# An attention and expert-layer kernel: the product with v in two column tiles, and the sums of the exponentials on GpSimd

## The chip, the cores and the metric

The kernel runs on one core of a Trainium2 chip. The metric is the device time of one execution in microseconds (us). TensorE (PE, with PEld for its weight loads) multiplies matrices into PSUM; VectorE (DVE), ScalarE (ACT) and GpSimd (POOL) work element by element; SyncE (SP) issues most of the transfers (DMA).

## What is computed

Clustered attention, followed by two multiplicative layers. The part that matters here is the end of the attention:

```python
mask = q_assign[:, :, :, None] == k_assign[:, :, None, :]
scores = scale * np.matmul(q, k.transpose(0, 1, 3, 2))
scores = np.where(mask, scores, -1000000000.0)
scores = scores - np.max(scores, axis=-1, keepdims=True)
attn = np.exp(scores)
attn = attn / (np.sum(attn, axis=-1, keepdims=True) + 1e-09)
return np.matmul(attn, v).astype(np.float32)
```

There are 2 batches of 8 heads, so 16 heads, with 768 queries and keys and 64 columns of v each. The result, as 1536 rows of 512, goes through `(x @ w1) * (x @ w2) @ w3 @ w_out` and then `softplus(x @ w_in) @ w_out2`. Everything is float32.

## The kernel before

The program has three stages. A preparation reads the first heads. A loop over slots (`for s in range(NSLOT + ML + AL)`, L897) does the attention, six slots to a head (QC = 6), 96 slots of work and ten to fill and empty the pipeline; beside it runs the product of w3 and w_out, in steps of a table (`w_step`), and the preparation of the next pair of heads (`steps`). Then come the two layers, l1 and l2 first (L965), l3 and l4 after.

In slot s the loop issues, in this order: the minimum products of slot s (`mx_pe`) and their reduction on VectorE (`mx_red`); the score products of slot j = s - 9 (`st_pe`) into the bank `sb`, and their exponential on ScalarE (`st_exp`) into a tile E; the product with v of slot a = s - 10 (`av_pe`) into the bank `avb`. Each of `mb`, `sb` and `avb` is one buffer, so the next slot's products wait until its reader has finished. E has two buffers.

A slot of scores covers 256 keys (two tiles i of 128) and 384 queries, one half hf; three slots make a half. The array holds 128 columns for `av_pe`: 64 of v and 64 of ones (`load_v` sets them by a memset on GpSimd), so that one half of the rows of `avb` holds the product and the other the sum of the exponentials:

```python
for i in range(2):
    nc.tensor.matmul(avbank[:, :HALF], V[g][:, 2 * kp + i, :], e[:, i, :],
        start=(kp == 0 and i == 0), stop=(kp == 2 and i == 1))
```

`av_ev` copies `avb` to a tile t on ScalarE, twice a head. The sums then go through DRAM: `r_ev` issues on SyncE sd<-t (twice), r<-sd, then rd<-r behind a reciprocal of 128 x 6 on VectorE, then R<-rd, which spreads the reciprocals over 64 rows. `x_norm` multiplies t by R on GpSimd, into XT.

The order of the work is written out by hand in the loop; each engine runs its own instructions in order, and waits for what the others must have finished. Behind the loop the weights of l1 are decoded (ACT, DVE, POOL in turn, `feed.take`) and XT is split into tiles xs (`split_x`), which share the four buffers of the pool xp with the tiles of v.

Of the kernel before, what the change touches and what calls it, by code (L numbers as in the profile page):

```python
# [8 lines left out]
F32 = mybir.dt.float32  # L9
# [18 lines left out]
def fused_kernel(ctx: ExitStack, tc, q, k, v, centroids, w1, w2, w3, wo, w_in, w_o2, out):  # L28
# [6 lines left out]
    nc = tc.nc  # L35
    B, H, S, D = q.shape
# [3 lines left out]
    QC = S // P  # L40
    HALF = S // 2
# [29 lines left out]
    cpool = pool(ctx, "cpool")  # L71
    dma_in = nc.sync.dma_start
# [51 lines left out]
    nc.vector.memset(ones, 1.0)  # L124
    half_c = cpool.tile([P, 1], F32, name="half_c")
    nc.vector.memset(half_c, 0.5)
    wfirst = cpool.tile([P, NCL], F32, name="wfirst")
    for c in range(NCL):
        nc.vector.memset(wfirst[:, c : c + 1], float(NCL - c))
# [37 lines left out]
                yield slice(lo - o, hi - o), XT[b][:, c, lo - b * S : hi - b * S]  # L167

    w12e = pool(ctx, "w12e", bufs=4, side="right")
    ep = pool(es_att, "ep", bufs=2, side="right")  # L170
    sp = pool(es_att, "sp", bufs=2, side="right")
    w3p = pool(es_att, "w3p", bufs=2, side="right")
    drp = pool(es_att, "drp", bufs=2, space=DRAM)


    xp = pool(ctx, "xp", bufs=4)
# [384 lines left out]
    NWSTEP = 3 * NW + 10  # L561

    def load_v(pi):

        if pi < NPAIR:
            b, h0 = divmod(2 * pi, H)
            for j in range(2):
                t = xp.tile([P, QC, 2 * D], F32, tag="x", name=f"v{pi}_{j}")
                nc.gpsimd.memset(t[:, :, D * (1 - j) : D * (2 - j)], 1.0)
                dma_in(  # L570
                    t[:, :, D * j : D * j + D], v[b, h0 + j].rearrange("(p c) d -> p c d", p=P)
                )
                V[2 * pi + j] = t


    PE = {
# [13 lines left out]
    NH = B * H  # L590
    NSLOT = NH * QC
    ML = 9
    AL = 1
    MN, E, TT, R = {}, {}, {}, {}


    def mx_pe(s):
# [24 lines left out]

    def st_pe(j):
        g, r = divmod(j, QC)
        hf, kp = divmod(r, 3)
        qs = slice(hf * HALF, (hf + 1) * HALF)
        for i in range(2):
            ks = slice((2 * kp + i) * P, (2 * kp + i + 1) * P)
            for n in range(2):
                nc.tensor.matmul(  # L630
                    sbank[:, i, :HALF], KT[g][: P - 31 * n, n, ks],
                    QT[g][: P - 31 * n, n, qs], start=(n == 0), stop=(n == 1),
                )

    def st_exp(j):
# [3 lines left out]
    def av_pe(j):  # L639

        g, r = divmod(j, QC)
        kp = r % 3
        e = E.pop(j)
# [6 lines left out]
    def av_ev(u):  # L650
        g, hf = divmod(u, 2)
        j = g % 2
        t = TT[u] = sp.tile([P, HALF], F32, tag="t", name=f"t{u}", bufs=5)
        act_copy(t, avbank[:, :HALF])
        if hf == 0:
            R["s", g] = drp.tile([2, HALF], F32, tag="sd", name=f"sd{g}")
        o = D * (1 - j)
        nc.sync.dma_start(R["s", g][hf : hf + 1, :], t[o : o + 1, :])

    def r_ev(g, i):  # L660

        pi, j = divmod(g, 2)
        if i == 0:
            R["t", g] = sp.tile([P, 2, QC], F32, tag="r", name=f"r{g}")
            nc.sync.dma_start(
                R["t", g][:, 0], R.pop(("s", g)).rearrange("h (a x) -> (h a) x", x=QC)
            )
        elif i == 1:
            t = R.pop(("t", g))
            nc.vector.tensor_scalar(  # L670
                out=t[:, 0], in0=t[:, 0], scalar1=1e-9, scalar2=None, op0=ALU.add
            )
            nc.vector.reciprocal(t[:, 1], t[:, 0])
            R["d", g] = drp.tile([2, HALF], F32, tag="rd", name=f"rd{g}")
            nc.sync.dma_start(R["d", g].rearrange("h (a x) -> (h a) x", x=QC), t[:, 1])
        else:
            if j == 0:
                R[pi] = sp.tile([P, S], F32, tag="R", name=f"R{pi}")
            nc.sync.dma_start(
                R[pi][D * j : D * j + D, :],  # L680
                R.pop(("d", g)).rearrange("h n -> (h n)").partition_broadcast(D),
            )

    def x_norm(u):
        g, hf = divmod(u, 2)
# [158 lines left out]
    with tc.manual_schedule():  # L844
        act_dma = nc.scalar.dma_start
        load_qk(0, [0])
        load_qk(0, [1], act_dma)
        nc.scalar.preload_act_table_set("natural_log_exp_and_others")
        centroid_load()
        for _ in range(3):  # L850
            w_load()
        centroid_prep()
        t1_pe(0, 0)
        t1_pe(0, 1)
        t1_ev(0, 0)
# [24 lines left out]
        assign(0, 1)  # L880
        w_step(0, "A")
        wk[0] = 1
        back_pe(0)
        back_ev(0)
        m_dma(0, 0, act_dma)
        m_dma(0, 1, act_dma)
        for r in range(-20, -2 * QC):
            steps(PE, r + 2 * QC)
            steps(EV, r + 2 * QC)
            if r % 2 == 0:  # L890
                w_next()
                w_next()
        while wk[0] < W0:
            w_next()
        load_v(0)
        load_v(1)
        for s in range(NSLOT + ML + AL):  # L897
            j = s - ML
            a = j - AL
            if s < NSLOT:  # L900
                mx_pe(s)
                mx_red(s)
            if s and s % QC == 0 and s <= NSLOT:
# [19 lines left out]
            for g in range(NH):
                r = s - (ML + AL + QC * g + QC - 1)
                if r in (2, 4, 6):
                    r_ev(g, r // 2 - 1)
                if r == 8:
                    x_norm(2 * g)
                    x_norm(2 * g + 1)
# [5 lines left out]
    av_ev(2 * NH - 1)  # L935
    for g in range(NH):
        r0 = NSLOT + ML + AL - (ML + AL + QC * g + QC - 1)
        for r in (2, 4, 6):
            if r >= r0:
                r_ev(g, r // 2 - 1)  # L940
        if 8 >= r0:
            x_norm(2 * g)
            x_norm(2 * g + 1)
# [167 lines left out]
```

## Time and profile before

| | us |
|---|---|
| median of 3 runs (lowest, highest) | 858.82 (856.37, 859.01) |
| the profiled execution | 859.42 |
| its span | 857.6 |
| of it before the loop's steady part, 0 to 55 | 55 |
| the loop over heads, 55 to 387 | 332 |
| the layers, 387 to 857.6 | 470.6 |

Over the whole span PE is busy 94%, PEld 74%, DVE 58%, ACT 46% and POOL 28%. Matmuls are pipelined, so the record of one overlaps the next; what a matmul costs in a row of them is read from the chain of waits, which gives each piece only the time that it adds. A line such as L645 names the place in the program. A row of a group gives the instruction, what it writes and reads, its shape and count, the busy time, the mean duration in ns, and the idle time just before it with what ended it.

### The profile page before, as it was taken

The page shows a single profiled execution, that of the slowest core. Times are in us where ns is not written, and L with a number is a line of the kernel's source. Part 1 is how long each engine was busy: PE and PEld are TensorE (multiplying, and loading weights), DVE is VectorE, ACT ScalarE, POOL GpSimd, SP SyncE. Part 2 cuts the span into 40 slices and gives each one's busy share as a digit, 9 for nine tenths or more (in the row PEclk, how much of TensorE's full clock was granted, in tenths as well). Part 3 has the DMA queues.
Part 4 walks back from the last instruction along what each step waited for, and adds up shares of the span by engine and source line. Part 5 has one row for each costly group of instructions (what it writes and reads, how often), then busy time and mean ns, then how long its engine had stood idle before and what let it go on. Part 6 is the DMA issues. An engine that isn't in the chain of part 4 may idle for free.

```text
span 857.6 us, 10092 instructions
## 1 busy us (share of the span) xinstructions
PE 802.5 (94%) x3553; PEld 637.9 (74%) x3553; DVE 495.6 (58%) x823; ACT 396.4 (46%) x683; POOL 243.6 (28%) x229
## 2 busy tenths in 40 slices
PE   4269999998999999989999999999999999999997
PEld 3157777776777777758888888887877788888886
DVE  5675657674776664438543254553988644454442
ACT  3324444554443444455443235454564644455443
POOL 2241214261424111135411113231344222222221
PEclk9979999998999999999999999999999999999999
DMA  8585474577445364025511114340120000001001
GB/s 211 136 185 147 101 178 115 147 164 171 120 111 120 84 157 109 15 69 183 170 49 50 50 50 147 99 147 1 50 74 1 23 28 1 0 1 50 1 1 50
DMA packets 77827, 76.40 MB, mean 89 GB/s; under 512 B 46416, under 2 KB 62928, under 8 KB 77776
## 3 DMA queue, kind: packets, MB, share of 16 engines
q1 hardware_dynamic: 72880, 74.17, 32.3%
q10 hardware_dynamic: 4896, 1.57, 1.0%
q8 instruction: 28, 0.46, 0.2%
q14 instruction: 23, 0.19, 0.1%
HBM read 50.41 MB, written 3.24 MB: 63 GB/s over the span
## 4 chain that ended last, share of the span: by engine, by line
PE 78%; DVE 9%; ACT 3%; SPq 3%; DMA 3%; issue 2%; POOL 1%; ACTq 0%; DVEq 0%; POOLq 0%
PE avb L645 13%; PE rb L793 8%; PE sb L793 8%; PE sb L630 7%; PE sb L999 6%; PE mb L1042 6%; PE rb L999 5%; PE rb L515 5%; PE mb L815 4%; PE mb L600 4%; PE rb L1042 3%; PE avb L1042 3%; PE avb L815 2%; PE rb L815 2%; PE rb L353 2%
## 5 line engine op out<-in xcount | busy, mean ns | idle before, releaser
L609 DVE TENSOR_REDUCE mn<-mb 128x1 f32<-128x768 f32 x96 | 91.8, 956 | 95.4 <-PE mb L600 95.2
L645 PE MATMUL avb<-E,v 128*128 128x384 f32 x384 | 143.1, 495 | 1.4 <-ACT t L61 1.3
L66 POOL TENSOR_TENSOR u<-u,t 128x512 f32<-128x512 f32 x48 | 68.5, 1427 | 170.1 <-DVE u L1022 170.1
L637 ACT ACTIVATE E<-sb 128x768 f32<-128x768 f32 x96 | 77.7, 810 | 68.7 <-PE sb L630 67.2
L630 PE MATMUL sb<-q,k 128*128 128x384 f32 (+1 forms) x384 | 92.2, 363 | 9.2 <-ACT E L637 9.2
L645 PEld LDWEIGHTS avb<-E,v 128*128 128x128 f32 x384 | 71.9, 193 | 30.8 <-ACT t L61 4.4
L600 PE MATMUL mb<-k,q 128*128 128x384 f32 x192 | 70.0, 447 | 16.6 <-DVE mn L609 16.1
L630 PEld LDWEIGHTS sb<-q,k 128*128 128x128 f32 (+1 forms) x384 | 67.6, 195 | 16.2 <-ACT E L637 13.0
L999 PE MATMUL sb<-ys,wh_i 128*128 128x512 f32 x192 | 64.1, 395 | 3.6 <-ACT t L1010 2.3
L600 PEld LDWEIGHTS mb<-k,q 128*128 128x128 f32 x192 | 36.0, 201 | 36.7 <-DVE mn L609 21.2
L999 PE MATMUL rb<-ys,wh_i 128*128 128x512 f32 x192 | 63.4, 392 | 0.0
L793 PE MATMUL rb<-xs,wh 128*128 128x512 f32 x192 | 61.6, 392 | 0.0
L793 PE MATMUL sb<-xs,wh 128*128 128x512 f32 x192 | 61.6, 392 | 0.0
L1012 DVE TENSOR_SCALAR u<-t 128x512 f32<-128x512 f32 x48 | 21.4, 446 | 66.8 <-ACT t L1011 66.8
L66 POOL TENSOR_TENSOR wl_o<-d_o,wh_o 128x512 fp32r<-128x512 f32 x16 | 21.6, 1350 | 121.2 <-ACT wh_o L61 121.2
L69 DVE TENSOR_TENSOR gl<-u,gh 128x512 fp32r<-128x512 f32 x48 | 39.6, 825 | 19.6 <-ACT gh L61 19.1
L692 POOL TENSOR_TENSOR xT<-t,R 64x384 f32<-64x384 f32 x32 | 34.7, 1102 | 46.8 <-DMA R<-rd 37.1
L1021 ACT ACTIVATE u<-u 128x512 f32<-128x512 f32 x48 | 30.4, 633 | 35.6 <-DVE t L1018 35.4
L999 PEld LDWEIGHTS sb<-ys,wh_i 128*128 128x128 f32 x192 | 35.9, 188 | 13.6 <-ACT t L1010 3.4
L333 POOL MEMSET k<- 1x768 f32 x16 | 11.8, 744 | 107.6 <-issue 83.2
L999 PEld LDWEIGHTS rb<-ys,wh_i 128*128 128x128 f32 x192 | 36.1, 188 | 8.0
L793 PEld LDWEIGHTS sb<-xs,wh 128*128 128x128 f32 x192 | 36.1, 188 | 7.8
(175 smaller groups left out, 1798.7 us busy)
## 6 DMA issues: line engine op xcount, KB each, us to landing
w3r<-in_moe_w_dram SPq DMA_DIRECT2D x16, 512.0 KB
w12r<-in_moe_w_dram SPq DMA_DIRECT2D x16, 512.0 KB
wir<-in_moe_w_in_dram SPq DMA_DIRECT2D x16, 512.0 KB
wor<-in_moe_w_out_dram SPq DMA_DIRECT2D x16, 512.0 KB
q<-H SPq DMA_DIRECT2D x16, 384.0 KB
w3r<-in_moe_w_out_dram SPq DMA_DIRECT2D x8, 512.0 KB
k<-H SPq DMA_DIRECT2D x16, 192.0 KB
k<-L SPq DMA_DIRECT2D x16, 192.0 KB
```

Of the source, the lines that this page charges most:

```text
L66: nc.gpsimd.tensor_tensor(out=o, in0=i, in1=hi, op=ALU.subtract)
L69: return nc.vector.tensor_tensor(out=o, in0=i, in1=hi, op=ALU.subtract)
L515: nc.tensor.matmul(m, a[:, ks], bb, start=(mc == 0 and x == 0), stop=(mc == NK - 1 and x == 2))
L600: nc.tensor.matmul(mbank[:, hf, :HALF], QT[g][:, 0, c * P : (c + 1) * P], KT[g][:, 0, hf * HALF : (hf + 1) * HALF], start=True, stop=True,)
L609: nc.vector.tensor_reduce(out=MN[g][:, c : c + 1], in_=mbank[:, :, :HALF], op=ALU.min, axis=AX.XY)
L630: nc.tensor.matmul(sbank[:, i, :HALF], KT[g][: P - 31 * n, n, ks], QT[g][: P - 31 * n, n, qs], start=(n == 0), stop=(n == 1),)
L637: nc.scalar.activation(E[j], sbank[:, :, :HALF], AF.Exp, scale=-1.0)
L645: nc.tensor.matmul(avbank[:, :HALF], V[g][:, 2 * kp + i, :], e[:, i, :], start=(kp == 0 and i == 0), stop=(kp == 2 and i == 1),)
L793: nc.tensor.matmul(bk[:, :BLK], a[:, sl], bb, start=(n == 0), stop=(n == 3 * CC - 1))
L815: nc.tensor.matmul(ybank[e][:, :BLK], a[:, es], bb, start=(fc == 0 and n == 0), stop=(fc == NFC - 1 and n == 2),)
L999: nc.tensor.matmul(hbank[(bl * NF2 + fc) % 4][:, :BLK], a[:, sl], bb, start=(n == 0), stop=(n == 3 * CC - 1))
L1042: nc.tensor.matmul(ob, a[:, sl], bb, start=(fc == 0 and n == 0), stop=(fc == NF2 - 1 and n == 2),)
```

## The change

The product with v uses v alone, 64 columns wide. A slot now covers 128 keys and all 768 queries, and its two products, one for each half of the queries, write rows 0 to 63 and 64 to 127 of `avb`. The memsets of ones in v go. The sums are made apart: GpSimd adds the six E of a head (`es_add`, five adds of 128 x 768), TensorE multiplies the result with a tile of ones (`sum_pe`, two products of 64 columns a head), and ScalarE copies them and adds 1e-9 (`sum_ev`). The reciprocals are taken on all 128 rows, in three instructions of 128 columns a head (`r_ev`). The DRAM tiles and the five transfers a head go. E has four buffers; the sums share the pool xp with v and xs.

```diff
-    ep = pool(es_att, "ep", bufs=2, side="right")
+    ep = pool(es_att, "ep", bufs=4, side="right")
...
+            t = xp.tile([P, 2, QC, D], F32, tag="x", name=f"v{pi}")
+            dma_in(t, v[b, h0 : h0 + 2].rearrange("h (p c) d -> p h c d", p=P))
             for j in range(2):
-                t = xp.tile([P, QC, 2 * D], F32, tag="x", name=f"v{pi}_{j}")
-                nc.gpsimd.memset(t[:, :, D * (1 - j) : D * (2 - j)], 1.0)
...
+                V[2 * pi + j] = t[:, j]
...
     def st_pe(j):
         g, r = divmod(j, QC)
-        hf, kp = divmod(r, 3)
-        qs = slice(hf * HALF, (hf + 1) * HALF)
-        for i in range(2):
-            ks = slice((2 * kp + i) * P, (2 * kp + i + 1) * P)
-            for n in range(2):
+        ks = slice(r * P, (r + 1) * P)
+        for n in range(2):
+            for i in range(2):
                 nc.tensor.matmul(
                     sbank[:, i, :HALF], KT[g][: P - 31 * n, n, ks],
-                    QT[g][: P - 31 * n, n, qs], start=(n == 0), stop=(n == 1),
+                    QT[g][: P - 31 * n, n, i * HALF : (i + 1) * HALF],
+                    start=(n == 0), stop=(n == 1),
                 )
...
         for i in range(2):
             nc.tensor.matmul(
-                avbank[:, :HALF], V[g][:, 2 * kp + i, :], e[:, i, :],
-                start=(kp == 0 and i == 0), stop=(kp == 2 and i == 1),
-            )
...
+                avbank[D * i : D * i + D, :HALF], V[g][:, r, :], E[j][:, i, :],
+                start=(r == 0), stop=(r == QC - 1),
+            )
+
+    def es_add(j):
...
+        nc.gpsimd.tensor_tensor(out=ES[g], in0=a, in1=e, op=ALU.add)
...
+    def sum_pe(g):
...
+        for i in range(2):
+            nc.tensor.matmul(m[D * i : D * i + D, :HALF], ones, e[:, i, :], start=True, stop=True)
+
+    def sum_ev(g):
+        m = R.pop(("b", g))
+        R[g] = sp.tile([P, HALF], F32, tag="R", name=f"R{g}")
+        nc.scalar.activation(R[g], m[:, :HALF], AF.Identity, bias=epscol[:, 0:1])
+        give(m)
...
+        t = R[g][:, i * P : (i + 1) * P]
+        nc.vector.reciprocal(t, t)
...
+    def head_end(g, r, part):
+
+        if part == 0:
+            if r == 1:
+                av_ev(g)
+            if r == 3:
+                sum_ev(g)
+        elif part == 1:
+            if r == 2:
+                sum_pe(g)
+        else:
+            if r in (3, 4, 5):
+                r_ev(g, r - 3)
+            if r == 7:
+                x_norm(g, 0)
+                x_norm(g, 1)
...
             if 0 <= a:
                 av_pe(a)
+                es_add(a)
+            for x in ends:
+                head_end(*x, 1)
```

Here r counts the slots since the last product of head g.

On TensorE, late in the loop where no w3 products are left, three slots read like this before (mb holds the minimum products, sb the scores, avb the product with v; x2 and x4 count instructions, the last figures are rows out x columns):

```order
L600 MATMUL mb_98<-k15_2661,q15_2660 128x384 x2
L630 MATMUL sb_97<-q13_2366,k13_2367 128x384 x4
L645 MATMUL avb_99<-E82_2842,v6_1_2507 128x384 x2
L600 MATMUL mb_98<-k15_2661,q15_2660 128x384 x2
L630 MATMUL sb_97<-q14_2575,k14_2576 128x384 x4
L645 MATMUL avb_99<-E83_2857,v6_1_2507 128x384 x2
```

and like this now, around the sums of head 12:

```order
L625 MATMUL sb_99<-q13_2347,k13_2348 128x384 x4
L639 MATMUL avb_101<-E78_2757,v6_2487 64x384 x2
L597 MATMUL mb_100<-k14_2554,q14_2553 128x384 x2
L625 MATMUL sb_99<-q13_2347,k13_2348 128x384 x4
L639 MATMUL avb_101<-E79_2771,v6_2487 64x384 x2
L666 MATMUL rb2_104<-es12_2698,ones_65 64x384 x2
L597 MATMUL mb_100<-k15_2639,q15_2638 128x384 x2
```

The products with v have 64 rows out and stand between products of 128, and once a head two more of 64 follow them.

On GpSimd, in the same part of the loop, a head had the two products of `x_norm`, the memsets of v and one memset of k before:

```order
L692 TENSOR_TENSOR xT1_2467<-t20_2495,R5_2691 64x384
L692 TENSOR_TENSOR xT1_2467<-t21_2568,R5_2691 64x384
L569 MEMSET v7_0_2745 128x6x64
L569 MEMSET v7_1_2748 128x6x64
L692 TENSOR_TENSOR xT1_2467<-t22_2631,R5_2691 64x384
```

Now five adds stand between the products of two heads:

```order
L686 TENSOR_TENSOR xT1_2429<-t10_2547,R10_2596 64x384 x2
L655 TENSOR_TENSOR es12_2698<-E72_2667,E73_2681 128x768
L655 TENSOR_TENSOR es12_2698<-es12_2698,E74_2694 128x768
L655 TENSOR_TENSOR es12_2698<-es12_2698,E75_2716 128x768
L655 TENSOR_TENSOR es12_2698<-es12_2698,E76_2731 128x768
L655 TENSOR_TENSOR es12_2698<-es12_2698,E77_2744 128x768
L686 TENSOR_TENSOR xT1_2429<-t11_2675,R11_2706 64x384 x2
```

Each add follows its E, and frees it.

On TensorE at the end of the loop, l1 (xs times wh and wl) followed the last product with v before:

```order
L793 MATMUL rb0_100<-xs0_0_3061,wh1_0_3051 128x512
L645 MATMUL avb_99<-E95_3019,v7_1_2748 128x384 x2
L793 MATMUL sb_97<-xs0_0_3061,wh0_0_2931 128x512
L793 MATMUL sb_97<-xs0_0_3061,wl0_0_2932 128x512
L793 MATMUL sb_97<-xs0_0_3061,wh0_0_2931 128x512
```

Now the sums of the last head stand within its first products:

```order
L804 MATMUL rb0_102<-xs0_0_3037,wh1_0_3027 128x512
L639 MATMUL avb_101<-E95_2995,v7_2725 64x384 x2
L804 MATMUL sb_99<-xs0_0_3037,wh0_0_2906 128x512
L666 MATMUL rb1_103<-es15_2965,ones_65 64x384 x2
L804 MATMUL sb_99<-xs0_0_3037,wl0_0_2907 128x512
```

## Rows read from the trace of the kernel before

**Rows 1.** Stretches of the span: length, each engine's busy us, clock, DMA share, GB/s

```profile
core 0: us, PE busy (x) PEld busy (x) DVE busy (x) ACT busy (x) POOL busy (x), PEclk, DMA share, GB/s
55.00:387.00 332.00, 318.77 (x1456) 244.14 (x1456) 202.25 (x336) 159.53 (x268) 97.40 (x110) 0.97 0.50 122
133.85:157.22 23.37, 23.35 (x111) 17.85 (x110) 16.13 (x28) 11.41 (x20) 6.55 (x7) 1.00 0.45 111
177.07:194.53 17.46, 17.01 (x80) 12.43 (x79) 15.55 (x26) 10.45 (x18) 12.19 (x11) 1.00 0.60 145
221.44:245.02 23.58, 23.56 (x113) 17.84 (x112) 18.26 (x32) 11.46 (x21) 6.55 (x7) 1.00 0.50 122
196.00:207.00 11.00, 7.65 (x23) 5.12 (x23) 4.39 (x9) 3.31 (x6) 2.45 (x4) 0.75 0.65 167
```

**Rows 2.** Chain of waits, pieces of the loop: start us, us, what

```profile
145.72 0.44 PE rb L496 x4
...
295.27 2.78 PE rb L515 x12
...
358.52 0.35 PE mb L600 x2
358.87 0.70 PE sb L630 x4
359.57 1.29 PE avb L645 x4
360.86 0.11 PE rb L616
```

**Rows 3.** Timeline of PE and PEld, same slots: start, duration, instruction, count

```profile
142.79 0.81 PE L600 MATMUL mb<-k,q 128*128 128x384 f32 x2
...
143.09 0.19 PEld L600 LDWEIGHTS mb<-k,q 128*128 128x128 f32 x1
143.26 0.08 PEld L616 LDWEIGHTS rb<-identF,mn 128*6 128x6 f32 x1
...
359.41 1.45 PE L645 MATMUL avb<-E,v 128*128 128x384 f32 x4
```

**Rows 4.** DVE groups (busy, mean ns), then L465's durations, least, median, most, 55:387

```profile
L673 DVE RECIPROCAL r<-r 128x6 f32<-128x6 f32 x16 | 3.0, 190 | 0.5
L297 DVE RECIPROCAL nrm<-nrm 128x24 f32<-128x24 f32 x8 | 2.4, 302 | 0.3
...
L465 DVE TENSOR_SCALAR w3r<-w3r 128x512 int32<-128x512 int32 x20 | 14.1, 705 | 0.0
...
L465 DVE TENSOR_SCALAR w3r<-w3r x20: 417/514/1236, 57.4 to 267.3; 128x512 int32<-128x512 int32 x20
```

**Rows 5.** POOL groups (busy, mean ns), and L692's durations

```profile
L256 POOL TENSOR_TENSOR sq<-rawqk 128x768 f32<-128x768 f32 x12 | 17.7, 1474 | 9.8 <-DMA rawqk<-in_q_dram 9.1
L266 POOL TENSOR_TENSOR sq<-sq 128x384 f32<-128x384 f32 x12 | 12.8, 1066 | 0.9
L266 POOL TENSOR_TENSOR sq<-sq 128x192 f32<-128x192 f32 x12 | 8.2, 680 | 0.9
...
L692 POOL TENSOR_TENSOR xT<-t,R x32: 992/1008/1555, 118.5 to 409.5; 64x384 f32<-64x384 f32 x32
```

**Rows 6.** Who waited for whom, 55:387: us in total, times, longest us

```profile
SPq L658 <- ACT t L61: 42.5, 17, 7.1
...
SPq L679 <- DMA rd<-r: 11.8, 6, 3.7
...
ACT H L318 <- DMA k<-H: 6.4, 2, 3.9
```

**Rows 7.** Timeline of one score round, and the first l1 products in the chain

```profile
354.03 0.86 PE L630 MATMUL sb<-q,k 128*128 128x384 f32 x4
...
354.99 0.81 ACT L637 ACTIVATE E<-sb 128x768 f32<-128x768 f32 x1 [1.53 <-PE sb L630]
...
386.93 5.57 PE sb L793 x24
```

More of the change, by code (lines that the diff above doesn't have):

```diff
@@ L126, in fused_kernel @@
     nc.vector.memset(half_c, 0.5)
+    epscol = cpool.tile([P, 1], F32, name="epscol")
+    nc.vector.memset(epscol, 1e-9)
     wfirst = cpool.tile([P, NCL], F32, name="wfirst")
@@ L169, in fused_kernel @@
     w12e = pool(ctx, "w12e", bufs=4, side="right")
-    ep = pool(es_att, "ep", bufs=2, side="right")
+    ep = pool(es_att, "ep", bufs=4, side="right")
     sp = pool(es_att, "sp", bufs=2, side="right")
     w3p = pool(es_att, "w3p", bufs=2, side="right")
-    drp = pool(es_att, "drp", bufs=2, space=DRAM)
     xp = pool(ctx, "xp", bufs=4)
@@ L566, in load_v @@
             b, h0 = divmod(2 * pi, H)
+            t = xp.tile([P, 2, QC, D], F32, tag="x", name=f"v{pi}")
+            dma_in(t, v[b, h0 : h0 + 2].rearrange("h (p c) d -> p h c d", p=P))
             for j in range(2):
-                t = xp.tile([P, QC, 2 * D], F32, tag="x", name=f"v{pi}_{j}")
-                nc.gpsimd.memset(t[:, :, D * (1 - j) : D * (2 - j)], 1.0)
-                dma_in(
-                    t[:, :, D * j : D * j + D], v[b, h0 + j].rearrange("(p c) d -> p c d", p=P)
-                )
-                V[2 * pi + j] = t
+                V[2 * pi + j] = t[:, j]
     PE = {
@@ L593, in fused_kernel @@
     AL = 1
-    MN, E, TT, R = {}, {}, {}, {}
+    MN, E, ES, TT, R = {}, {}, {}, {}, {}
     def mx_pe(s):
@@ L641, in av_pe @@
         g, r = divmod(j, QC)
-        kp = r % 3
-        e = E.pop(j)
         for i in range(2):
             nc.tensor.matmul(
-                avbank[:, :HALF], V[g][:, 2 * kp + i, :], e[:, i, :],
-                start=(kp == 0 and i == 0), stop=(kp == 2 and i == 1),
-            )
[L650 to L653, printed above, removed]
-        act_copy(t, avbank[:, :HALF])
[L655 to L658, printed above, removed]
@@ L660, in r_ev @@
-    def r_ev(g, i):
[L662 to L682, printed above, removed]
@@ L684, in x_norm @@
-    def x_norm(u):
-        g, hf = divmod(u, 2)
+                avbank[D * i : D * i + D, :HALF], V[g][:, r, :], E[j][:, i, :],
+                start=(r == 0), stop=(r == QC - 1),
+            )
+    def es_add(j):
+        g, r = divmod(j, QC)
+        if r == 0:
+            return
+        e = E.pop(j)
+        if r == 1:
+            ES[g] = xp.tile([P, 2, HALF], F32, tag="x", name=f"es{g}")
+            a = E.pop(j - 1)
+        else:
+            a = ES[g]
+        nc.gpsimd.tensor_tensor(out=ES[g], in0=a, in1=e, op=ALU.add)
@@ new lines, in av_ev @@
+    def av_ev(g):
+        t = TT[g] = sp.tile([P, HALF], F32, tag="t", name=f"t{g}", bufs=3)
+        act_copy(t, avbank[:, :HALF])
+    def sum_pe(g):
+        m = R["b", g] = take()
+        e = ES.pop(g)
+        for i in range(2):
[5 more added lines that the diff above has]
+        give(m)
@@ L686, in x_norm @@
+    def r_ev(g, i):
+        t = R[g][:, i * P : (i + 1) * P]
+        nc.vector.reciprocal(t, t)
+    def x_norm(g, hf):
         b, h = divmod(g, H)
@@ L690, in x_norm @@
         rs = slice(D * (h % 2), D * (h % 2) + D)
-        cs = slice(hf * HALF, (hf + 1) * HALF)
+        hs = slice(D * hf, D * hf + D)
         nc.gpsimd.tensor_tensor(
-            out=XT[b][rs, h // 2, cs],
-            in0=TT.pop(u)[rs], in1=R[g // 2][rs, cs], op=ALU.mult,
-        )
+            out=XT[b][rs, h // 2, hf * HALF : (hf + 1) * HALF],
+            in0=TT[g][hs], in1=R[g][hs], op=ALU.mult,
+        )
+    def head_end(g, r, part):
+        if part == 0:
+            if r == 1:
+                av_ev(g)
[4 more added lines that the diff above has]
+                sum_pe(g)
+        else:
+            if r in (3, 4, 5):
[3 more added lines that the diff above has]
+                x_norm(g, 1)
     w12p = w12q = abp = w34a = raws2 = decp = None
@@ L902, in fused_kernel @@
                 mx_red(s)
+            g, r = divmod(a - QC + 1, QC)
+            ends = [(x, r + QC * (g - x)) for x in range(max(0, g - 1), min(NH - 1, g) + 1)] if g >= 0 else []
+            for x in ends:
+                head_end(*x, 0)
             if s and s % QC == 0 and s <= NSLOT:
@@ L907, in fused_kernel @@
                 w_step(wk[0], "hlpqe")
-            if a > 0 and a % 3 == 0:
-                av_ev(a // 3 - 1)
             steps(PE, s)
@@ L918, in fused_kernel @@
                 av_pe(a)
+                es_add(a)
+            for x in ends:
+                head_end(*x, 1)
             if weights:
@@ L921, in fused_kernel @@
                 wk[0] += 1
[L923 to L929, printed above, removed]
+            for x in ends:
+                head_end(*x, 2)
             if wk[0] == NWSTEP:
@@ L934, in fused_kernel @@
                 taken += 2
[L935 to L943, printed above, removed]
+    for r in range(1, 8):
+        for part in range(3):
+            head_end(NH - 2, r + QC, part)
+            head_end(NH - 1, r, part)
     es_prep.close()
```

## The prediction

> **What bounds the kernel now.** I read the stages first, then the chain of waits inside the attention loop, then each engine's rows. The profiled execution took 859.42 us: a span of 857.6 and 1.8 around it, 0.6 above the median of the three runs (858.82). The change touches only the loop over heads, 332 us of the span from 55 to 387. There the tensor engine is busy for 318.8 of 332 us, VectorE for 202, GpSimd for 97 [rows 1]. So the loop is set by what TensorE issues, and the reader should see how one slot of it adds up: in the chain, the two minimum products take 0.35, the four score products 0.70, the product with v 1.29 [rows 2], together 2.34 us. Behind the last w3 product, which starts at 295.27 [rows 2], slots hold next to nothing else; I call these 33 (E63 to E95) the light slots. Two heavier kinds lie before: heads with two w3 products of 2.78 each [rows 2], lasting 23.4 and 23.6 us, and the head from 177.07 to 194.53, where TensorE is busy 17.0 of 17.5 but VectorE already 15.6 and GpSimd 12.2 [rows 1].
>
> **The change, part by part.** *Product with v.* Its 96 slots cost 96 x 1.29 = 124 us. Each of the two products of a slot is two matmul records of 0.32. Now each fills one half of the columns. If the halves run side by side, a slot pays 0.645 and the loop gains 62 us; if they run one after the other, nothing. No row shows two half-width matmuls. Taken in program order, the second record of the first half can share its time with the first record of the second half, but the two records of one half can't overlap: 3 x 0.32 = 0.97, gain 31 us. It lies midway between the ends and I take it.
>
> The Trainium skill, "TensorE: Matmul & The Clock Gate", Part 3, reports 2.38 times the speed for three column tiles. By that ratio two would give about 1.6, an estimate of 0.81 per slot and 46 us gained; no run here shows it yet.
>
> *Sums.* 16 x 2 products of the same shape with ones: 16 x 0.97 = +15.5 us (10 to 21).
>
> *Switching.* A slot now goes from full to half width and back, as do the sums: 2 x (96 + 16) = 224 switches. The nearest row is the small transpose of the minima, six columns between full-width neighbours: it costs 0.11 on the chain, as much as one of the four full ones in 0.44, and its weights load while the matmul before it runs [rows 2, 3]. That says 0. The other end: the array must empty first, which costs the tail of a record beyond its step (1.45 - 1.29 = 0.16) plus a weight load that nothing covers (0.19) [rows 2, 3], 0.35 in all, 78 us. I take half a tail, 0.08, so +18 us, because the six-column row is a single pass and may not be a narrower mode at all.
>
> TensorE alone: -31 + 15.5 + 18 = +2.5 us, with ends at -52 and +99.
>
> *VectorE.* Out go 16 pairs of tiny instructions; in come 48 reciprocals of 128 columns. 6 columns cost 0.19, 24 cost 0.30, so about 6 ns a column: 0.93 us each, 45 us in all, 38 net (0.30 to 0.93 each as ends: 8 to 38), or 2.4 per head. Other work there gets longer too: the shift L465 takes 0.42 at best, up to 1.24, and 0.71 in the mean, 0.29 above the best [rows 4]; its long cases lie beside GpSimd work, and in a heavy head GpSimd is busy 28% of the time [rows 1]. With the adds that becomes 65% (below), so I take 0.29 x 65 / 28 = 0.67, 0.38 more, for each of the seven steps per head that read SBUF the same way (two weight pieces of three, one small): +2.7, say 3 us (0 to 5). So VectorE needs 5.4 more per head: 16.1 becomes 21.5 of 23.4 in the first heavy heads, 18.3 becomes 23.7 against 23.6 in the four of the second group, 15.6 becomes 21.0 against 17.5 in the one head without w3 products [rows 1]. Cost beyond TensorE: 4 x 0.5 + 3.5 = +5.5. Behind a late reciprocal stand the next minimum reduction and with it the next minimum products on TensorE.
>
> *GpSimd.* 80 adds of 768 columns. 192 columns take 0.68 and 384 take 1.07, so 768 about 1.82 (1.47 is the floor, from the square of 768) [rows 5]: 146 us, 9.1 per head, less the 6 us of memsets that go. Heavy heads hold 6.6 now, so 15.3 of 23.4; the 177 us head 21.3 of 17.5, the same excess as VectorE's and not counted twice. The four buffers of E let the adds lag three slots, so I cost them at nothing; if that cover fails, see the last rival.
>
> *DMA.* The five small transfers per head through DRAM go, 80 issues, and with them SyncE's waits, 42.5 and 11.8 us in the two lines shown [rows 6]. Most delayed nobody; the stall at 196 to 207, where TensorE stands for 3.35 of 11 us and the clock falls to 0.75 behind a wait for a copy of k [rows 1, 6], should shrink: -3 (0 to -5).
>
> *The end.* The last sum product now stands behind the last add (1.8) and a weight split on GpSimd, and the fourth xs tile waits for it, while l1 has eight matmuls of 0.23 to cover that [rows 7]. +4 (0 to 7).
>
> Sum: 2.5 + 5.5 - 3 + 4 = +9, so 859.4 + 9 = **868 us**.
>
> **The rivals.** *Side by side and free (faster).* Halves at 0.645, switches at 0, as the six-column row suggests. TensorE would drop to 19.7 in a heavy head, but VectorE then sets 22 of 23.4 in the first three and a half (-5) and 23.7 in the second group (+0.5). Light slots can't go below the round of the score bank: record 0.86, exp 0.81, two hand-overs of about 0.09 [rows 7], so 1.84 instead of 2.34: 33 x 0.5 = -16.5. With +3.5 for the 177 us head, -3 and +4: **843 us**. For it: nothing in the trace shows a switch cost, and the two halves share no column. Against: no evidence of overlap either, and the gain is capped by VectorE.
>
> *Every switch empties the array (slower).* 0.35 each, 78 us. With halves at 0.645: -62 + 10 + 78 = +26, with 0.97: +62; +1 from DMA and end. 887 to 923, middle **905 us**. It decides from 0.07 a switch if halves cost 0.97, from 0.23 if 0.645. For it: records outlast their step by 0.16, and weights load before their matmul, which an emptied array can't do [rows 3]. Against: the six-column transpose.
>
> The Trainium skill, "TensorEngine Tiling (Array Packing)", Tiling Modes, states that changing the tiling mode drains TensorE. It speaks for this rival; the six-column row does not agree, if it counts as a mode.
>
> *GpSimd holds E (slower).* The products of x_norm on GpSimd stretch from 0.99 to 1.56 [rows 5]. Adds stretched alike take 2.85: 14.2 + 2 = 16.3 in a light head against 14.0, so exp waits for a free E, 5.5 x 2.3 = +13: **881 us**.
>
> **How the numbers follow.** Forecast (858 to 880) 0.37; side by side (836 to 852) 0.35; emptied array 0.20; GpSimd 0.08. One measurement tells about 0.3% from no change. Of the forecast 0.10 lies within that (856.2 to 861.4), 0.02 below, 0.25 above. Faster: 0.35 + 0.02 = 0.37; same 0.10; slower 0.25 + 0.20 + 0.08 = 0.53. The range goes from 838 to 905: it leaves out the lowest tenth of the faster case's 0.35 and the upper half of the emptied array's 0.20, and holds all else. Because both signs carry much, the forecast's own range, 858 to 880, stands beside it.
>
> **What would show it.** The step from the first av record of a slot to the next full-width matmul in the chain: 0.65, 0.97 or 1.29, plus a gap on either side if switching costs. VectorE's share in the heads of the second group near 95%; 0.93 us per reciprocal; adds of 1.8; fewer light-slot microseconds than 2.34 only if the halves overlap. The prediction is wrong if light slots take 1.9 or less (faster), or over 2.7 (slower), or if exp waits on GpSimd.

## The result, and the profile after

The changed kernel takes 867.61 us in the median of its runs (866.15 to 874.62) against 858.91 (856.37 to 859.81) for the kernel before: a ratio of 1.0128, with a 95% interval from 1.0101 to 1.0156. The forecast was 868. The profiled execution took 868.74, with a span of 866.9, 9.3 more than before.

Four marks say where the 9.3 us came from: the first exp, the first exp of head 11, the last exp, and the first product of l2, behind which both kernels run the same program. Starts, durations and instructions of the last three; of before (the last line is from the chain of waits):

```profile
311.77 0.81 ACT L637 ACTIVATE E<-sb 128x768 f32<-128x768 f32 x1 [2.86 <-PE sb L630]
384.21 0.81 ACT L637 ACTIVATE E<-sb 128x768 f32<-128x768 f32 x1 [0.99 <-PE sb L630]
403.16 0.68 PE avb L815 x3
```

and of after:

```profile
312.01 0.81 ACT L633 ACTIVATE E<-sb 128x768 f32<-128x768 f32 x1 [2.58 <-PE sb L625]
379.58 0.81 ACT L633 ACTIVATE E<-sb 128x768 f32<-128x768 f32 x1 [0.56 <-PE sb L625]
412.44 0.68 PE avb L826 x3
```

The first exp starts at 65.24 before and at 64.84 after. So:

| us | before | after | difference |
|---|---|---|---|
| to the first exp | 65.24 | 64.84 | -0.4 |
| heads 0 to 10 | 246.53 | 247.17 | +0.6 |
| heads 11 to 15, to the last exp | 72.44 | 67.57 | -4.9 |
| last exp to the first l2 product | 18.95 | 32.86 | +13.9 |
| the rest | 454.44 | 454.46 | 0.0 |

The product with v became much cheaper, heads 0 to 10 did not become shorter in sum, the light ones did by a little, and all of that and more was lost at the end of the loop. Nor is all of the 4.9 in heads 11 to 15 TensorE's: heads 12 and 13 lost 1.2 each, but 2.9 lie in head 15, of which 2.1 are in one slot, where ScalarE of before stood for a load of l1's weights with the exp behind it (the step from one exp to the next was 4.27, and is 2.13 now). The chain of before:

```profile
370.50 5.50 DMA w12r<-in_moe_w_dram
...
376.64 0.83 ACT E L637
```

**The light slots.** The chain of waits shows a light slot of after (start, us, what), then the sums of a head and the first piece of the next slot:

```profile
330.43 0.55 PE mb L597 x2
330.98 0.69 PE sb L625 x4
331.67 0.80 PE avb L639 x4
332.46 0.65 PE rb L666 x4
333.11 0.55 PE mb L597 x2
```

A slot is 0.55 + 0.69 + 0.80 = 2.04 instead of 2.34. Read against [rows 2]: the product with v fell from 1.29 to 0.80, but the minimum products behind it rose from 0.35 to 0.55. The two sum products (four records) take 0.65 behind a product with v, where nothing changes width: two times 0.32, so two halves run side by side and share all of their time. The product with v should then also cost 0.645; I take the other 0.155 for the way into half width, and the 0.20 on the minimum products for the way back (e4 tests their sum, 0.35). The timeline of PE and PEld shows the way back where a full product follows:

```profile
380.64 0.87 PE L639 MATMUL avb<-E,v 128*64 128x384 f32 x4
381.43 0.19 PEld L804 LDWEIGHTS sb<-xs,wh 128*128 128x128 f32 x1 [0.60 <-issue]
```

The weight load stands until the narrow products are nearly through (0.60 in which it waited for nothing that the profile names); before, weights for the next product were loaded while the last one ran [rows 3].

**The heavy heads.** Busy time by engine (columns as in [rows 1]) in the whole loop, in a heavy head of the first group, in one of the second, and in a light head:

```profile
55.00:387.00 332.00, 299.82 (x1514) 190.81 (x1513) 257.80 (x350) 161.21 (x268) 241.12 (x174) 0.96 0.45 111
133.75:157.12 23.37, 22.12 (x118) 14.26 (x116) 20.21 (x30) 11.57 (x21) 19.70 (x16) 1.00 0.49 115
...
219.53:246.56 27.03, 23.40 (x122) 14.63 (x120) 23.20 (x35) 11.59 (x20) 21.18 (x17) 1.00 0.52 122
...
327.70:340.67 12.97, 12.97 (x67) 7.48 (x67) 8.33 (x10) 6.15 (x10) 12.42 (x9) 1.00 0.51 124
```

Head 7 (219.53) lasts 27.0 us where it lasted 23.6, and neither TensorE, 23.4, nor VectorE, 23.2, is busy throughout: they wait for one another. Part of the answer is in how long single steps of VectorE last (least, median, most, in ns, from 55 to 330). Before:

```profile
L469 DVE SCALAR_TENSOR_TENSOR w3r<-w3r x20: 628/656/1462, 59.2 to 274.3; 128x512 int32<-128x512 int32 x20
L281 DVE TENSOR_SCALAR nrm<-nrm x6: 178/178/179, 64.6 to 291.6; 128x24 f32<-128x24 f32 x6
```

After:

```profile
L470 DVE SCALAR_TENSOR_TENSOR w3r<-w3r x20: 627/678/2181, 58.8 to 273.9; 128x512 int32<-128x512 int32 x20
L475 DVE SCALAR_TENSOR_TENSOR w3d<-w3r x20: 677/720/2302, 61.7 to 278.4; 128x512 int32<-128x512 int32 x20
L282 DVE TENSOR_SCALAR nrm<-nrm x6: 178/990/1143, 64.2 to 291.7; 128x24 f32<-128x24 f32 x6
```

L282 works on 24 columns and needs 0.18 us; now it lasts 0.99 in the median. The timeline of after shows why (start, us, instruction):

```profile
105.98 3.84 POOL L655 TENSOR_TENSOR es<-es,E 128x768 f32<-128x768 f32 x2
...
108.71 1.14 DVE L282 TENSOR_SCALAR nrm<-nrm 128x24 f32<-128x24 f32 x1
109.77 2.36 POOL L686 TENSOR_TENSOR xT<-t,R 64x384 f32<-64x384 f32 x2
...
110.27 0.79 ACT L633 ACTIVATE E<-sb 128x768 f32<-128x768 f32 x1
```

The two adds end at 109.82, and L282, begun at 108.71, ends at 109.85. Behind it ScalarE takes the roots and only then the exp at 110.27, so TensorE stands too. A longer step shows that this is a wait and not a slower rate:

```profile
229.25 1.81 POOL L655 TENSOR_TENSOR es<-es,E 128x768 f32<-128x768 f32 x1
229.41 2.21 DVE L475 SCALAR_TENSOR_TENSOR w3d<-w3r 128x512 int32<-128x512 int32 x1
```

The add ends at 231.06, and L475, which takes 0.68 at least, ends 0.56 behind it: nearly all of its own time was still to come. The long cases of L470 and L475 beside adds end 0.54 to 0.56 behind the add (one more overlaps two adds that are merged in the view), those of L466 about 0.3, those of L282 0.03.

TensorE also loses its clock; the next stretches of 4 us from 108:

```profile
108.00:112.00 4.00, 2.36 (x15) 1.72 (x13) 3.01 (x5) 2.08 (x6) 3.92 (x3) 1.00 0.92 217
112.00:116.00 4.00, 4.00 (x12) 2.55 (x12) 2.06 (x4) 1.76 (x3) 1.30 (x4) 0.57 0.52 136
```

TensorE was busy for 2.36 of 4 us, and in the next 4 us the granted clock is 0.57, most of the time its lower level of 1.2 GHz; twelve w3 products take 4.29 us there instead of 2.96, by the chain:

```profile
100.70 2.96 PE rb L516 x12
...
113.14 4.29 PE rb L516 x12
```

**The end.** The chain from the last multiplications of head 14 to l1 (in full, the waits say `PE rb L666 <- POOL es L655: 9.8, 1, 9.8`):

```profile
385.88 1.31 POOL xT L686
...
387.26 1.33 POOL xT L686
...
389.91 1.81 POOL es L655
391.72 0.04 issue
391.76 1.55 PE rb L666 x4
393.31 3.71 PE sb L804 x10
```

TensorE stands for 9.8 us before the last sum products. They need the last add, and the last add stands in GpSimd's queue behind x_norm of head 14, which waited 2.3 us for a reciprocal, and a weight split. The reciprocals in their turn stood behind three steps of VectorE that lasted 2.3 us each beside the adds. Then l1 begins at a lower clock (granted 0.50 from 388 to 392 and 0.52 from 392 to 396): ten products in 3.71 us, while before 24 took 5.57 [rows 7].

### The profile page after: what moved, and what is told of

Its sections match the earlier page's. It is cut to its first block, busy times and chain, and to the rows that moved or that the text cites. A ratio compares the mean times of both kernels' runs of the same rounds, so it can differ in the third digit from the quotient of the medians.

```text
span 866.9 us, 10205 instructions
## 1 busy us (share of the span) xinstructions
PE 788.4 (91%) x3617; PEld 585.9 (68%) x3617; DVE 553.0 (64%) x840; ACT 398.1 (46%) x683; POOL 391.9 (45%) x293
## 4 chain that ended last, share of the span: by engine, by line
PE 72%; DVE 17%; issue 3%; POOL 3%; ACT 3%; DMA 1%; SPq 1%; ACTq 0%; POOLq 0%; DVEq 0%
PE sb L804 8%; PE rb L804 8%; PE sb L1004 6%; PE mb L1047 6%; PE rb L1004 6%; PE rb L516 6%; PE avb L639 5%; PE sb L625 5%; PE mb L597 4%; PE mb L826 4%; DVE mn L606 3%; PE avb L1047 3%; PE rb L1047 3%; PE avb L826 2%; PE rb L826 2%
## 5 line engine op out<-in xcount | busy, mean ns | idle before, releaser
L66 POOL TENSOR_TENSOR u<-u,t 128x512 f32<-128x512 f32 x48 | 68.4, 1427 | 170.7 <-DVE u L1027 166.4
L655 POOL TENSOR_TENSOR es<-es,E 128x768 f32<-128x768 f32 x64 | 121.8, 1903 | 32.1 <-ACT E L633 29.6
L625 PE MATMUL sb<-q,k 97*128 97x384 f32 (+1 forms) x384 | 91.3, 361 | 13.9 <-ACT E L633 13.9
L639 PE MATMUL avb<-E,v 128*64 128x384 f32 x384 | 85.5, 525 | 0.0
L625 PEld LDWEIGHTS sb<-q,k 97*128 97x128 f32 (+1 forms) x384 | 67.3, 196 | 23.2 <-ACT E L633 21.6
L597 PE MATMUL mb<-k,q 128*128 128x384 f32 x192 | 60.5, 397 | 23.6 <-DVE mn L606 21.7
L597 PEld LDWEIGHTS mb<-k,q 128*128 128x128 f32 x192 | 31.9, 200 | 62.1 <-DVE mn L606 45.7
L677 DVE RECIPROCAL R<-R 128x128 f32<-128x128 f32 x48 | 44.9, 939 | 8.2 <-ACT R L671 8.2
L1004 PEld LDWEIGHTS sb<-ys,wh_i 128*128 128x128 f32 x192 | 35.9, 188 | 13.5 <-ACT t L1015 3.1
L804 PEld LDWEIGHTS rb<-xs,wh 128*128 128x128 f32 x192 | 36.1, 188 | 9.5 <-ACT ab L61 1.1
```

What stands on the lines that cost most here:

```text
L66: nc.gpsimd.tensor_tensor(out=o, in0=i, in1=hi, op=ALU.subtract)
L597: nc.tensor.matmul(mbank[:, hf, :HALF], QT[g][:, 0, c * P : (c + 1) * P], KT[g][:, 0, hf * HALF : (hf + 1) * HALF], start=True, stop=True,)
L625: nc.tensor.matmul(sbank[:, i, :HALF], KT[g][: P - 31 * n, n, ks], QT[g][: P - 31 * n, n, i * HALF : (i + 1) * HALF], start=(n == 0), stop ...
L639: nc.tensor.matmul(avbank[D * i : D * i + D, :HALF], V[g][:, r, :], E[j][:, i, :], start=(r == 0), stop=(r == QC - 1),)
L655: nc.gpsimd.tensor_tensor(out=ES[g], in0=a, in1=e, op=ALU.add)
L804: nc.tensor.matmul(bk[:, :BLK], a[:, sl], bb, start=(n == 0), stop=(n == 3 * CC - 1))
```

## Experiments

Times are medians, ratios are to the kernel before on the same chip; parts are as in the table above, from each profiled run.

| kernel | us | ratio (95%) | heads 0-10 | heads 11-15 | end |
|---|---|---|---|---|---|
| before | | | 246.5 | 72.4 | 19.0 |
| after | 867.6 | 1.0128 (1.0101, 1.0156) | 247.2 | 67.6 | 32.9 |
| e1 last sums on TensorE | 860.4 | 1.0043 (1.0011, 1.0074) | 253.7 | 73.7 | 19.3 |
| e2 no reciprocals | 868.5 | 1.0120 (1.0092, 1.0148) | 250.2 | 67.7 | 28.8 |
| e3 no adds | 848.3 | 0.9886 (0.9863, 0.9908) | 236.0 | 67.6 | 22.5 |
| e4 before, in two column tiles | 879.7 | 1.0249 (1.0233, 1.0264) | 259.2 | 79.6 | 19.7 |
| e5 neither adds nor reciprocals | 843.7 | 0.9834 (0.9798, 0.9870) | 230.6 | 67.4 | 19.2 |
| e6 e1, and L282 off VectorE | 857.7 | 0.9985 (0.9954, 1.0016) | 243.0 | 74.4 | 19.3 |
| e7 e1, and products in pairs | 875.2 | 1.0198 (1.0159, 1.0236) | 249.1 | 83.8 | 19.4 |
| e8 e6 and e7 | 875.0 | 1.0195 (1.0153, 1.0238) | 247.8 | 88.7 | 19.3 |
| e9 e6, and adds in halves | 853.0 | 0.9937 (0.9917, 0.9956) | 241.5 | 74.7 | 19.3 |
| e10 e6, and logarithm and exp | 850.5 | 0.9916 (0.9889, 0.9943) | 236.0 | 74.2 | 19.4 |
| e11 e6, e9 and e10 | 848.0 | 0.9887 (0.9866, 0.9907) | 235.7 | 70.9 | 19.4 |

Runs of one kernel scatter: ten of e1 go from 856.7 to 869.3, and its profiled one (868.3) is near the top, with a granted clock of 0.92 from 55 to 330 where the changed kernel has 0.96; the profiled one of e5 (839.1) is 4.6 below its median. The heads 0 to 10 of these two are not typical. The last column hardly scatters (19.3 to 19.4 in the seven kernels that end as e1 does).

### e1: the last head's sums without GpSimd

```diff
 def av_pe(j):
...
+    if g == NH - 1:
+        if r == 0:
+            R["b", g] = take()
+        m = R["b", g]
+        for i in range(2):
+            nc.tensor.matmul(m[D * i : D * i + D, :HALF], ones, E[j][:, i, :],
+                start=(r == 0), stop=(r == QC - 1))
```

with `es_add` and `sum_pe` doing nothing for that head.

> The changed kernel, but the sums of the last head (15) are taken by TensorE straight from each E, two more products of 64 columns beside each product with v in its six slots; GpSimd adds nothing for that head. In the changed kernel TensorE stands 9.84 us before the last sum products, and l1 reaches its first l2 product 13.9 us later, counted from the last exp, than before. Theory (GpSimd's queue holds the end): this goes, for about 1.5 us more in the last head, and l1 starts about 9 us earlier at full clock: 856 us, 11 below the changed kernel. Rival (the end waits for the split weights and the x tiles anyway): TensorE meets another wait of similar length, 863 us or more.

Measured 860.4. From the last exp to l2 it is 19.3 us, as before:

```profile
392.19 0.81 ACT L633 ACTIVATE E<-sb 128x768 f32<-128x768 f32 x1 [0.97 <-PE sb L625]
...
411.53 0.68 PE avb L840 x3
```

So GpSimd's queue is what the end cost, 13.5 of its 13.9 us. The last head pays 1.7 for it (12.8 against 11.2 from the first exp to the last), as expected. The total fell short, 7 us instead of 11, because heads 11 to 15 became longer by 6.1, 4.4 more than that: in head 11 (+3.3) a new wait appears, told under e6.

### e2, e3 and e5: adds and reciprocals, left out one by one and together

```diff
 def r_ev(g, i):
-    t = R[g][:, i * P : (i + 1) * P]
-    nc.vector.reciprocal(t, t)
+    return
```

> The changed kernel without the 48 reciprocals on VectorE (left out: the division, x_norm multiplies by the sums), all else as it is. Theory (VectorE sets the heavy heads, through the reciprocals' own 2.8 us a head): TensorE sets them again and heads 1 to 10 last about 22.2 instead of 23.4 to 27, so 10 to 13 us go there and 2 to 3 at the end: 852 us. Rival (it is the stretching of VectorE's steps beside GpSimd's adds, reciprocals fit in its gaps): under 5 us, 863.

```diff
 def es_add(j):
...
-    nc.gpsimd.tensor_tensor(out=ES[g], in0=a, in1=e, op=ALU.add)
+    ES[g] = E.pop(j)
```

> The changed kernel without the 80 adds on GpSimd (left out: five sixths of each sum; the sum products read the last E of a head). Theory as above (reciprocals bind the heavy heads, GpSimd's queue the end): 12 to 14 us go at the end, VectorE's shift and its two companions return from 0.77, 0.92 and 1.07 us to near their least, some 1.5 us a head, of which part shows: 850 us. Rival (the adds' contention is what binds the heavy heads): 843 us, with heavy heads at 22.2.

> The changed kernel without the adds on GpSimd and without the reciprocals on VectorE (both left out). Alone, leaving out the reciprocals gained nothing (868.5) and leaving out the adds 19 (848.3). Theory (a VectorE step that reads two SBUF operands or runs wide waits until the add on GpSimd ends, so the wait swallows what the reciprocals give back; without adds the reciprocals show): heads 5, 7 and 9, at 18.1, 24.2 and 23.1 us without adds, fall to about 17, 22.5 and 22: 843 to 845 us. Rival (reciprocals fit in VectorE's gaps in any case): 848.

My theory of the first two, that the reciprocals' 2.8 us a head set the heavy heads, fell: without the 45 us of reciprocals the time was 868.5, no change, which misses the theory's 852 and the rival's 863. It isn't that nothing moved: the end became 4.1 us shorter, and heads 0 to 10 3.0 longer. Without the adds it was 848.3, 19 less. That is near the theory's 850, but 10 of it lie at the end, where 12 to 14 were expected, and 11 in heads 0 to 10. The same place as above, in e2:

```profile
106.14 3.84 POOL L655 TENSOR_TENSOR es<-es,E 128x768 f32<-128x768 f32 x2
...
108.44 1.58 DVE L282 TENSOR_SCALAR nrm<-nrm 128x24 f32<-128x24 f32 x1
...
109.93 2.35 POOL L685 TENSOR_TENSOR xT<-t,R 64x384 f32<-64x384 f32 x2
```

Without the reciprocal ahead of it, L282 begins 0.27 earlier, lasts 0.44 longer, and ends with the adds (109.98) all the same: the time given back goes into the wait. In all, the five steps that lengthen beside adds (L282, L294, L466, L470, L475) are busy for 72.1 us from 55 to 330 in e2, 63.0 in the changed kernel, 42.4 without the adds and 46.6 before. With the adds gone, e5 is 4.6 us below e3 by the medians (0.5% by the ratios, whose intervals just overlap), within the 843 to 845 expected. But 3.3 of the 4.6 lie at the end (22.5 to 19.2), where x_norm of e3 waits 8.5 us for a reciprocal. Of the heads that were to show it only head 5 did so in full (17.1 instead of 18.1 us; 7 and 9 took 23.7 and 22.8 instead of 24.2 and 23.1, where 22.5 and 22 were expected), in a run faster than its median. So e5 does not show that reciprocals count in the heads; e10 below is the better evidence.

### e4: column tiles alone, in the kernel before

```diff
-    nc.tensor.matmul(
-        avbank[:, :HALF], V[g][:, 2 * kp + i, :], e[:, i, :],
+    for c in range(2):
+        cs = slice(D * c, D * c + D)
+        nc.tensor.matmul(
+            avbank[cs, :HALF], V[g][:, 2 * kp + i, cs], e[:, i, :],
...
```

> The kernel before, with each product with v (128 columns: v and ones) cut into two of 64 columns, one for v and one for ones, in the two halves of the array; nothing else differs. Theory (halves run side by side, and going to half width and back costs 0.15 + 0.20 a slot): light slots 2.69 instead of 2.34, in every slot, since TensorE sets the loop there: 859 + 96 x 0.35 = 892 us. Rival one (no switch cost; the 0.20 before the minimum products in the changed kernel has another cause): 859. Rival two (the halves share only part of their time, 0.97 for two): light slots 2.34 + 0.65 and more, 920 us or above.

The chain of a light slot:

```profile
345.10 0.55 PE mb L600 x2
345.65 0.70 PE sb L630 x4
346.35 1.44 PE avb L647 x8
347.79 0.55 PE mb L600 x2
```

0.55 + 0.70 + 1.44 = 2.69 us, as expected, and 1.44 = 0.155 + 2 x 0.645: the halves run side by side without loss, and a change there and back costs 0.35. In the whole it added 21 us, not 33: light heads 12 and 13 take 2.1 more each, six times 0.35, but heavy ones (1 to 3, 7 to 9) 1.5 to 1.8, and the stall in head 6 hid its share (24.0 instead of 26.9).

### e7 and e8: half as many changes of width

```diff
-    av_pe(a)
+    if a % 2:
+        av_pe(a - 1)
+        av_pe(a)
     es_add(a)
```

> The kernel with the last head's sums on TensorE, and the products with v of two slots issued together in every second slot: the same work, half as many changes between full and half width. Theory (a change there and back costs 0.35 us): light slots fall from 2.03 to 1.86 in the mean, in the 24 light slots and some of the heavy ones: 4 to 5 us fewer than 860.4, 856. Rival (the 0.35 is not the change of width but belongs to each slot's order): two slots stay at 4.06, 860.

> The two together: last head's sums on TensorE, products with v in pairs, the tiny step L282 taken off VectorE. Theory (the first saves in light heads, the second in heavy ones, so they add): 860.4 - 4.5 - 4.5 = 851 us. Rival (a shorter way on TensorE only lengthens its waits and lets its clock fall): 856 or more.

Both missed, on the slow side, 875: only e8's rival, 856 or more, covers it, and it gave another reason. The chain of a pair of light slots of e7:

```profile
335.54 1.44 PE avb L639 x8
336.98 0.56 PE mb L597 x2
...
337.57 0.97 DVE mn L606
...
338.58 0.62 PE mb L597 x2
...
339.20 0.96 PE sb L625 x4
340.16 1.44 PE avb L639 x8
```

Two products with v together take 1.44, not 2 x 0.80, so the price of the change is confirmed. But two slots take 4.62 instead of 4.07. In a slot without a product with v TensorE waits for the minimum reduction (one buffer `mb`), and the exp (one buffer `sb`) ends no earlier, at 339.13; the products with v had been the work beside which both ran. So the change of width was saved, and more was lost by waits that the moved product had covered.

### e6: one tiny step off VectorE

```diff
-    nc.vector.tensor_scalar_max(fl[:, 1], fl[:, 0], 1e-30)
-    nc.scalar.activation(fl[:, 2], fl[:, 1], AF.Ln)
+    nc.scalar.activation(fl[:, 2], fl[:, 0], AF.Ln, bias=tiny[:, 0:1])
```

> The kernel with the last head's sums on TensorE, and the tiny step L282 (max with 1e-30, 128x24, 0.18 us at its least, 0.77 in the mean beside the adds) taken off VectorE: ScalarE's logarithm adds 1e-30 itself. In the changed kernel the chain went through L282 for 1.15 us in three heads, with the next exp behind it. Theory (VectorE steps held up by an add, in the chain): 4 to 5 us fewer than the 860.4 of the kernel with the last sums alone, 856. Rival (the next step, L470 or L475 or the minimum reduction, takes its place): 860.

857.7: 2.7 us below e1 by the medians, 0.6% by the ratios, whose intervals just overlap; the way it was expected, but not clearly, and the 856 was not reached. The rival had a point: the other four steps (L294, L466, L470, L475 above, one line further on here) are busy for 65.8 us from 55 to 330, against 55.6 in e1 and 58.4 in the changed kernel. Its chain shows what stands in head 11 of e1, e6, e9 and e10 (18.5 to 19.0 us, against 15.7 in the changed kernel), a load of l1's weights:

```profile
301.06 12.04 DMA w12r<-in_moe_w_dram
...
313.72 0.82 ACT E L634
```

ScalarE and VectorE stand for the load in the middle of their queues, and the exp stands behind. In the changed kernel the same load is issued at 304.00, as far ahead of the first exp of head 11 as here (8.0 us), and is there before ScalarE asks for it at 313.15; here it takes longer. In e7 and e8 VectorE waits for it too (4.2 and 4.6 us). Why the load is late in these kernels was not tried.

### e9, e10 and e11: shorter adds, no reciprocals on VectorE

```diff
-    nc.gpsimd.tensor_tensor(out=ES[g], in0=a, in1=e, op=ALU.add)
+    for i in range(2):
+        nc.gpsimd.tensor_tensor(out=ES[g][:, i], in0=a[:, i], in1=e[:, i], op=ALU.add)
```

> The kernel of the root step (last head's sums on TensorE, L282 off VectorE), with each add on GpSimd cut into two of 384 columns: 1.07 us each by the rows, 2.14 for 1.82 together. Theory (a VectorE step waits until the add that runs ends, 2.2 us at the longest): the longest L470 and L475 fall from 2.2 to about 1.6, the heavy heads lose some of their waits, 1 to 4 us fewer than without the cut: 855 us. Rival (the two engines only share a port's rate, the step is slowed for as long as GpSimd is busy): GpSimd is busy longer, so steps get longer: 859 or more.

853.0, 4.7 below e6 (0.5% by the ratios, whose intervals just touch), though GpSimd is busy longer (205.9 us from 55 to 330, 194.7 in e6). The longest steps of VectorE:

```profile
L471 DVE SCALAR_TENSOR_TENSOR w3r<-w3r x20: 627/686/1491, 58.6 to 269.1; 128x512 int32<-128x512 int32 x20
L476 DVE SCALAR_TENSOR_TENSOR w3d<-w3r x20: 678/693/1502, 61.6 to 273.6; 128x512 int32<-128x512 int32 x20
```

They fell from 2.18 and 2.30 in the changed kernel (2.16 and 2.32 in e6) to 1.49 and 1.50, by 0.7 to 0.8, and an add from 1.90 to 1.08, by 0.8. The four steps named under e6 are busy for 53.3 us instead of 65.8. That is what a wait for the end of one add gives; a shared rate would have lengthened them.

```diff
-    nc.scalar.activation(R[g], m[:, :HALF], AF.Identity, bias=epscol[:, 0:1])
+    nc.scalar.activation(R[g], m[:, :HALF], AF.Ln, bias=epscol[:, 0:1])
+    nc.scalar.activation(R[g], R[g], AF.Exp, scale=-1.0)
```

with `r_ev` empty.

> The kernel of the root step, with the reciprocals taken off VectorE: ScalarE takes the logarithm of the sums (with 1e-9) and then the exponential of its negative, 0.58 us more a head on ScalarE, 2.8 less on VectorE. Theory (while adds run, the waits for them swallow what the reciprocals give back, as when they were left out alone): at most 2 us, 856 to 858. Rival (with L282 gone VectorE's own time counts, as it did without adds, 4.6 us): 853.

> Both together: halved adds, and reciprocals by logarithm and exponential on ScalarE. Theory: the two add, 853 to 856 us, since shorter adds leave less wait for the freed time to fall into. Rival (what is left is TensorE's work, its changes of width and its clock): as the better of the two alone.

e10 took 850.5, 7 below e6: my theory (at most 2) fell and the rival was nearer. With L282 off VectorE most of the freed time no longer goes into waits: the four steps rise by 2.6 us, from 65.8 to 68.4, where in e2 the five rose by 9.1. e11 took 848.0, 1.1% less than the kernel before (0.9866 to 0.9907), and beats both kernels. It was expected at 853 to 856; as its interval overlaps that of e10, it stays open whether the two add or the better one stands alone. Its profiled span is 10.8 us shorter than that of before: 10.8 and 1.5 less in heads 0 to 10 and 11 to 15, 0.5 more at the end and 1.1 more ahead of the first exp.

The Trainium skill, "SBUF — State Buffer", Who interferes with whom, states that VectorE's second port is GpSimd's only one, that it is held for a whole instruction, and that the other then blocks fully rather than slows down; it names steps with two inputs in SBUF and the wide modes of `tensor_scalar` as the ones that ask for it. The traces here agree: L282 and L466 (`tensor_scalar`) and L470 and L475 (two inputs) finish only behind the add that they meet, while the reciprocal, with one input, took 0.94 in the mean and 0.96 at most in the same stretch.

## Why the prediction came out right, and where it was wrong

The time was right to 0.4 us, and that is luck: the mechanisms were not, and two errors of about 20 us cancelled.

- **What bounds the loop.** TensorE's pieces sum to a light slot, and the light slots shortened by what the pieces did. Right. For the heavy heads it was true before the change only. And not all of the 33 light slots hold "next to nothing else": in heads 14 and 15 of before l1's weights hold up two exps, by slots of 4.49 and 4.27.
- **Product with v, -31.** The step that failed: "the two records of one half can't overlap", hence 0.97. The halves share all their time, 0.645 (e4, and the sum products at 0.65). The term is -62, the end of my range that I did not take. The ratio of the Trainium skill ("TensorE: Matmul & The Clock Gate", Part 3) gave an estimate of 0.81. The measured 0.80 is near it by chance, as it contains 0.155 for the change of width.
- **Sums, +15.5.** For the same reason 16 x 0.65 = +10.4.
- **Switches, +18.** I took 0.08 each, half a record's tail, for 224. Measured: 0.155 in and 0.20 out, so 0.175, within the ends 0 and 0.35; and 192 of them, since the sums stand beside a product with v and change nothing. 96 x 0.35 = +34. The six-column transpose pays no such price (0.11, and the score products behind it 0.70), so it was no guide, as I had suspected. The Trainium skill's rule that a change of tiling mode drains TensorE ("TensorEngine Tiling (Array Packing)", Tiling Modes) fits the 0.35 a slot. The price was half of the full drain that I had put into the second rival.
- TensorE in all: -62 + 10.4 + 34 = **-18** instead of +2.5. Of this the light heads 12 and 13 show their share in full, 1.2 each; heads 11 to 15 together show 4.9, with the 2.1 that are ScalarE's.
- **VectorE, +5.5, and GpSimd, 0.** The sizes of single instructions were right: a reciprocal 0.94 (forecast 0.93), an add 1.90 (1.82). The steps beside them became longer by 16 us in 55 to 330, some 1.4 a head, half of the 3 forecast; and the 4 x 0.5 was more than its own rows give (23.7 against 23.6). The step that failed was to compare busy time with the length of a head. A step that waits for an add does so at its place in the chain, in front of an exp or a minimum reduction. Heads 0 to 10 should have lost some 11 x 1.15 = 12.7 us by TensorE (6 x 0.30 less 0.65 a head), and gained 0.6 instead; without adds they are 11 us shorter (e3), without reciprocals no shorter (e2). And I asked whether the adds make the exp wait for a free E, not whom they hold up: ScalarE waited for GpSimd's use of E for under 2 us in all.
- **DMA, -3.** The stall did shrink: TensorE stands for 1.93 us at 196.5 where it stood for 3.35. But the clock falls there as before, and head 5 became longer: heads 5 and 6 together went from 44.4 to 41.9, which is hardly more than TensorE's own 2 x 1.15. So no gain beyond that is shown.
- **The end, +4.** The mechanism was named ("behind the last add (1.8) and a weight split"), the size was 13.9: I counted one add and a split, where GpSimd had a queue of adds, x_norm of head 14 and that one's wait for VectorE, and left out the lower clock after a stand. Without the adds 10.4 of the 13.9 go (e3), without the reciprocals 4.1 (e2).
- **The rivals.** "Side by side and free" was half true: side by side, not free. "Emptied array" was true in kind and half in price. "GpSimd holds E" did not occur; GpSimd holding VectorE did, and no rival said so. (In the first rival TensorE's 19.7 should be about 20.1 by its own terms, 23.4 - 3.9 + 0.65; nothing hung on it.) Of the marks for being wrong none was met: light slots took 2.04, between 1.9 and 2.7, and exp did not wait on GpSimd. The marks were too far apart to tell my forecast from what happened; the chain's 0.80 and 0.55 told at once.

What stays open: how much of heads 0 to 10 is the wait itself and how much the fall of the clock behind it. Between the first exp and the last, the changed kernel shows 4 such falls (at 72, 112, 200 and 368), the kernel before 2 (at 200 and 378), and one less the granted clock, times the length, is 1.5 to 3.4 us for each. In heads 0 to 10 that makes 6.8 after and 3.4 before, so by this estimate the clock itself has some 3 of the 13 us lost there, and waits the rest; but no run held the clock fixed.

## To carry to other kernels

Work moved to GpSimd is not free because GpSimd is idle: here VectorE steps of the kinds named above waited for the running add to end. So look for which of these stand in front of the bounding engine, take the tiny ones off VectorE, and cut the GpSimd instructions short. Narrow products side by side paid in full here, but each change of width had a price, and a product that is moved or shortened may have been the cover of another buffer's round. And at the end of a loop count what stands in the queue of the engine that now feeds the next stage, with the waits of its entries, not only the last entry.

## What was not expected of the hardware

Two 64-column f32 products in the two halves of the array took 0.645 together, as long as one of 128 columns, also when both read the same moving data (e4). Going to half width cost 0.155 us and coming back 0.20, and the weights of the next product were not loaded meanwhile. A VectorE step of 0.18 us lasted up to 1.14, and one of 0.68 up to 2.30, because they finished only behind the GpSimd add of 1.9; with adds of 1.08 the latter lasted 1.50 at most. After 4 us in which TensorE was busy for 2.36, its granted clock was 0.57 over the next 4.
